# Twelve direct second products of the second layer become block products, with weights and x prepared beside the first layer

## The chip, the cores and the metric

The kernel runs on one core of one Trainium2 chip. A core has a matrix engine (TensorE, PE in the profile, with its weight loads as PEld), three engines for elementwise work (VectorE = DVE, ScalarE = ACT, GpSimd = POOL) and SyncE (SP), which here issues the transfers (DMA). The metric is the time of one execution in device microseconds (us). A time is the median of the runs shown; the profile is of one execution.

## The reference

Causal attention with a decay over 4 x 8 heads of 576 rows and width 64 gives 2304 tokens of width 512. Two layers follow, each 512 to 2048 to 512, with a gate between its two products:

```python
attn_out = _attn_ref(**attn_kwargs)                      # 2304 x 512
h = x @ w_in                                             # first layer
g = s * (r * r) + b                                      # r = max(h, 0)
x = g @ w_out
h = x @ w_in                                             # second layer, other weights
g = np.maximum(h, 0.0) + alpha * np.minimum(h, 0.0)
return g @ w_out
```

The weights arrive as 64-bit floats, handed over as 64-bit integers; everything else is float32.

## The kernel before, in words

**Numbers.** TensorE multiplies operands rounded to a shorter format (fp32r), so each float32 operand is held as a high half (a rounded copy) and a low half (what the copy lost, by a subtraction), and each product is three matmuls: high x high, high x low, low x high. Forming a pair of halves is a copy, mostly by ScalarE, and a subtraction by VectorE or GpSimd.

**Three parts.** Until about 335 us the core computes attention, with the first layer of the first six token blocks (256 tokens each) over the first half of d_ff beside it. From 335 to 601 us it computes the rest of the first layer in "wide" steps (`moe_step` with `big`): one step takes one block of 128 rows of d_ff and 512 tokens (256 for the last block), with 12 matmuls for the first product (L968), then ScalarE's max (L972), VectorE's square and scale (L975), ScalarE's or VectorE's addition of b into the high half of g (L979, L981), VectorE's low half (L985), and 12 matmuls for the second product (L992 for 256 tokens, L995 for 512). There are 56 such steps, 40 of 512 tokens and 16 of 256. From 601 us the second layer runs: three passes over 768 tokens each, and in a pass eight steps p, each a pair of 128-row blocks of d_ff.

**The second layer's first product** (`pair`, L1271) is a 2 x 2 block product done with seven products instead of eight: seven operands of x (sums and differences of quarters), seven of the weights, 7 x 6 matmuls of 384 columns (L1290), and the sums of the seven results by ScalarE's copies and VectorE's additions (L1305, L1311) around the gate (L1314).

**Its second product** has two forms. `flat` (L1366) multiplies directly: 36 matmuls of 512 columns (L1382) a step, with the gate's result split into halves (L1340, L1344). `seconds` (L1153) takes the steps of a chunk (two or four) and makes seven block products of them, 9 matmuls of 256 columns (L1232) for each step and product; it needs combinations of g (L1159), their halves (L1216, L1218), seven weight operands a step, and additions of the results (L1173, L1257). PLAIN = (8, 4, 0) says how many steps of each pass use `flat`: all eight, four, none.

**The second layer's data.** Its weights are unpacked from 64 bits beside the first layer (`keep`, L477: ScalarE L456, VectorE L447, L450, L453) and stored as float32 in DRAM. In the first pass they are fetched again, and `sums_of` (L488) and `outs_of` (L525) form the seven operands of the first product and the halves of the direct one; `mixed_of` (L545), in the second pass, forms the four sums for the block products. Each x leaves `finish_x2` (L1019) as seven operands: split and subtracted in pieces (L1060, L1063, L1070), written to DRAM, and read again.

**The order.** The program is written out by a list scheduler in the kernel (`Scheduler`). Every piece of work is a task with its engine or engines, a modelled cost, the keys it reads and writes, its buffers and a priority (smaller goes first). The scheduler simulates the engines; each engine, when free, takes the ready task of the smallest priority whose buffers are free. Work that may go to VectorE or GpSimd is modelled with a shared port. Buffers come from rings with a fixed number of slots. The elementwise work has the priority EPR = -50, the wide steps 1000 and up, the weights of the second layer 1100 and up. On the chip each engine then runs its list in that order, waiting on semaphores.

## Time and profile before

| | |
|---|---|
| median of 3 runs (981.89 to 985.65) | 985.58 us |
| the profiled execution | 984.31 us |
| its span in the trace | 982.5 us |
| TensorE busy | 965.5 us (98%), 6063 matmuls |
| VectorE, ScalarE, GpSimd busy | 741.0, 529.9, 327.5 us |
| DMA | 219.34 MB, mean 223 GB/s |

The span is from the first to the last instruction that the profile shows; the rest of an execution, 1.8 us here, lies around it. Busy time counts an engine's own instructions only; a busy engine is not by itself the bound. A wait names the instruction that came last before the waiting one could go. A matmul's duration in the timeline is longer than the step from one start to the next, since matmuls overlap; the pace is read from starts.

### The profile page before, as it was taken

To read this page: it belongs to the slowest core of one execution; us is meant where nothing else is said; L and a number is where in the kernel's file an instruction comes from. 1 tells how busy PE (TensorE), PEld (TensorE's weight loads), DVE (VectorE), ACT (ScalarE), POOL (GpSimd) and SP (SyncE) were. 2 spreads that over 40 slices of the span, in tenths; PEclk is the share of its full clock that TensorE was granted. 3 is DMA by queue.
4 is the path that set the end of the run, shared out by engine and by line. 5 is a ranking of instruction groups with operands and counts; after the bars stand their busy time and mean duration, and the time that the engine had idled before them with its cause. 6 is when DMAs were issued, how large, how long until landed. Compare 5 with 4: busy or idle time off the path is not lost. (4 is left out here: it accounts for less than half of the span.)

```text
span 982.5 us, 17732 instructions
## 1 busy us (share of the span) xinstructions
PE 965.5 (98%) x6063; PEld 854.0 (87%) x6063; DVE 741.0 (75%) x1728; ACT 529.9 (54%) x1286; POOL 327.5 (33%) x369
## 2 busy tenths in 40 slices
PE   9999999999999999999999999999999999999997
PEld 6668898997998889988888887888989899999987
DVE  5888876577666488876878688999765779786597
ACT  4777766557566545443534444756535345455441
POOL 3655776375545034222000000454301112333023
PEclk8999999999999999999999999999999999999999
DMA  7764536233522444587798789788688988888645
GB/s 208 227 194 153 180 109 207 83 114 110 186 76 74 151 128 131 160 300 273 267 319 290 264 264 319 270 317 319 244 315 298 307 259 315 316 297 316 225 147 197
DMA packets 96079, 219.34 MB, mean 223 GB/s; under 512 B 8956, under 2 KB 50260, under 8 KB 93012
## 3 DMA queue, kind: packets, MB, share of 16 engines
q1 hardware_dynamic: 95988, 218.20, 65.9%
q8 instruction: 48, 0.79, 0.3%
q14 instruction: 43, 0.35, 0.1%
HBM read 143.45 MB, written 71.18 MB: 218 GB/s over the span
## 5 line engine op out<-in xcount | busy, mean ns | idle before, releaser
L968 PE MATMUL h<-x,i 128*128 128x256 f32 (+1 forms) x864 | 148.3, 320 | 0.3 <-DVE r L975 0.3
L968 PEld LDWEIGHTS h<-x,i 128*128 128x128 f32 x864 | 125.6, 189 | 13.2 <-DVE r L975 0.9
L826 POOL TENSOR_SCALAR e<-e,rec 128x128 f32<-128x128 f32 (+4 forms) x144 | 89.4, 632 | 85.4 <-DVE rec L819 35.5
L1382 PE MATMUL b<-wo,gq 128*128 128x512 f32 x432 | 103.7, 395 | 0.0
L992 PE MATMUL a<-g,o 128*128 128x256 f32 x768 | 103.6, 284 | 0.0
L992 PEld LDWEIGHTS a<-g,o 128*128 128x128 f32 x768 | 95.9, 189 | 1.2 <-issue 0.7
L1382 PEld LDWEIGHTS b<-wo,gq 128*128 128x128 f32 x432 | 80.9, 188 | 18.1
L995 PE MATMUL b<-g,o 128*128 128x512 f32 x384 | 94.4, 391 | 0.6 <-DVE g L985 0.6
L815 ACT ACTIVATE e<-e,ngm 128x128 f32<-128x128 f32 (+4 forms) x144 | 84.3, 587 | 14.8 <-DVE ngm L810 13.1
L1232 PE MATMUL b<-wo,gj 128*128 128x256 f32 x684 | 87.8, 285 | 2.6 <-ACT gj L1216 1.3
L1232 PEld LDWEIGHTS b<-wo,gj 128*128 128x128 f32 x684 | 86.1, 191 | 3.6 <-DVE gj L1218 1.6
L985 DVE SCALAR_TENSOR_TENSOR g<-r,small,g 128x256 fp32r<-128x256 f32 (+1 forms) x104 | 66.6, 640 | 26.8 <-ACT g L979 25.9
L995 PEld LDWEIGHTS b<-g,o 128*128 128x128 f32 x384 | 71.9, 188 | 16.7 <-DVE g L985 1.1
L979 ACT ACTIVATE g<-r,small 128x256 fp32r<-128x256 f32 (+1 forms) x90 | 53.5, 595 | 55.6 <-DVE r L975 22.0
L810 DVE CUSTOM_DVE_ANT_0 e<-s,mask 128x128 f32<-128x128 f32 (+4 forms) x144 | 67.2, 480 | 18.2 <-PE s L792 7.9
L517 POOL TENSOR_TENSOR wi<-sw,wi 128x512 fp32r<-128x512 f32 x12 | 18.3, 1542 | 173.5 <-ACT wi L514 170.1
L866 PE MATMUL t<-ident,e 128*128 128x128 f32 (+1 forms) x400 | 65.5, 277 | 3.5 <-ACT pt L875 2.1
L975 DVE SCALAR_TENSOR_TENSOR r<-h,small,r 128x256 f32<-128x256 f32 (+1 forms) x76 | 42.9, 564 | 34.5 <-ACT r L972 34.0
L877 ACT COPY pt<-t 128x256 f32<-128x256 f32 (+2 forms) x128 | 55.1, 451 | 20.0 <-PE t L866 19.4
L972 ACT ACTIVATE r<-h 128x256 f32<-128x256 f32 (+1 forms) x76 | 34.1, 449 | 53.4 <-PE h L968 53.0
L866 PEld LDWEIGHTS t<-ident,e 128*128 128x128 f32 (+1 forms) x400 | 46.9, 140 | 13.9 <-issue 5.8
L1290 PE MATMUL h<-x,wi 128*128 128x384 f32 x288 | 58.2, 338 | 0.3 <-DVE rt L1340 0.3
...
## 6 DMA issues: line engine op xcount, KB each, us to landing
...
```

The lines of the kernel that those rows point to most:

```text
L810: nc.vector.tensor_tensor_reduce(e.t[0:rows, k0:k1], st_.t[0:rows, 0:w], mask[0:rows, m0:m0 + w], -0.125 if u.f32 else -1.0, init, ALU.add ...
L815: nc.scalar.activation(x, x, AF.Exp, bias=ng[0:rows, col:col + 1], scale=-1.0, accum_out=sm[0:rows, col:col + 1])
L826: eng.tensor_scalar(x, x, rc[0:rows, col:col + 1], 1.0, ALU.mult, ALU.mult)
L866: nc.tensor.transpose(pp.t[0:kw, i * P:i * P + P], e.t[:, P * kb:P * kb + kw], ident)
L877: copy(x.t[0:kw, a:a + PTS * m].rearrange("p (m w) -> p m w", w=PTS)[:, :, 0:w], src)
L968: nc.tensor.matmul(ps.t[:, 0:w], wv[:, wl, kc, :], x.t[:, kc, xl, x0:x0 + w], start=(n == 0), stop=(n == 3 * KC - 1))
L985: nc.vector.scalar_tensor_tensor(g.t[:, 1, 0:w], r.t[:, 0:w], b_t, h, ALU.add, ALU.subtract)
L992: nc.tensor.matmul(acc[u // 2].t[:, T * (u % 2):T * (u % 2) + T], wo.t[:, wl, u * P:u * P + P], g.t[:, gl, 0:w], start=(first and i == 0 a ...
L995: nc.tensor.matmul(acc[u].t[:, 0:w], wo.t[:, wl, u * P:u * P + P], g.t[:, gl, 0:w], start=(first and i == 0), stop=end)
L1232: nc.tensor.matmul(y[t // 2].t[:, T * (t % 2):T * (t % 2) + T], g.t[:, gl, t * P:t * P + P], wop[j // 2].t.rearrange("p a n -> p (a n)").r ...
L1290: nc.tensor.matmul(b.t[:, 0:TH], wi.t[:, wop, wl, k * P:k * P + P], x[:, k, xl, :], start=(start and m == 0), stop=(m == 5), skip_group_ch ...
L1382: nc.tensor.matmul(y.t, G[e, h].t[:, gl, j * P:j * P + P], wo[e].t[:, wl, :], start=(m == 0), stop=(m == 5))
```

## The change

All 24 steps of the second layer take the block form of the second product; `flat`, PLAIN, `outs_of`, `sums_of` and `mixed_of` are gone. The steps are taken in chunks of 2, 2, 4 in the first pass, 4, 4 in the second, 4, 2, 2 in the third.

The seven operands of both weight matrices are formed beside the first layer by `seven_of`, one 256-column operand at a time with a store of its own (256 KB), and read again one by one. Two row pairs of the first matrix stay in SBUF (HELD), two others are formed in the second layer's first pass (LATE); twelve blocks are unpacked at 300 to 360 us already (EARLY).

In the wide steps of the first layer g is formed by ScalarE with four operations (max, square, scale and bias, rounded copy), and the low half is a subtraction on VectorE or GpSimd. The second product of a step is placed MM2 = 3.5 steps behind its first (2.5 before). The cost functions of the scheduler are new (`dv`, `ac`, `pl`).

x stays as float32: in SBUF (`xq`) for the first pass, by way of DRAM for the other two; its seven operands are formed where the pass begins, by operations of two times 384 columns (XOPS).

```diff
@@ -33,10 +33,14 @@
 NXE = 2
 CH = 4
-ZOFF = 0.0
-PLAIN = (8, 4, 0)
-CHUNKS = {1: (4, 6, 8), 2: (0, 4, 6, 8)}
-MIXED = {(1, 0): (3,), (1, 1): (2,), (1, 2): (1,), (1, 3): (0,), (1, 4): (4,), (1, 5): (5,), (1, 6): (6,), (1, 7): (7,)}
+KEEP = 2
+MM2 = 3.5
+LATE = [("wi2", p) for p in (6, 7)]
+EN = (8, 1)
+EA, EB = 300e3, 360e3
...
@@ -345,11 +365,11 @@
+    x2_d = [dram.tile([P, 2, 2, 2, TH], F32, name=f"x2_d{n}") for n in range(3)]
     w2i_d = [dram.tile([P, 7, 2, T], F32R, name=f"w2i_d{n}") for n in range(NP2)]
-    w2b_d = [dram.tile([P, CH, 2, 2, 512], F32R, name=f"w2b_d{n}") for n in range(NP2 // CH)]
-    w2t_d = [[dram.tile([P, CH, 2, T], F32R, name=f"w2t_d{n}_{i}") for i in range(4)] for n in range(NP2 // CH)]
+    w2o_d = [dram.tile([P, 7, CH, 2, T], F32R, name=f"w2o_d{n}") for n in range(NP2 // CH)]
...
@@ -386,16 +406,17 @@
-        "r2": ring("pg2", "r2", 2, [P, T2], F32),
-        "wi2": ring("w2", "wi2", 2, [P, 7, 2, T], F32R),
-        "wo2": ring("w2", "wo2", 4, [P, 2, 512], F32R),
+        "r2": ring("pg2", "r2", 3, [P, T2], F32),
+        "wq": ring("w2", "wq", 14, [P, 2, T], F32R),
+        "wp": ring("wp", "wp", 8, [P, 2, T], F32R),
+                "xq": ring("w2", "xq", 1, [P, 2, 4, TH], F32),
...
@@ -474,102 +501,94 @@
-    def keep(key, fc, prio):
+    SUMS = {"wi2": ((0, (1, 0), (1, 1), ALU.add), (2, (0, 0), (1, 0), ALU.subtract), (1, 0, (0, 0), ALU.subtract), (3, (0, 1), 1, ALU.subtract)),
+    WHOLE = {"wi2": ((0, 0), (0, 1), (1, 1)), "wo2": ((0, 0), (1, 0), (1, 1))}
...
+    def seven_of(key, p, prio, late=False):
...
+            fc, c = 2 * p + e, cb[e % len(cb)]
+            if (key, fc) in EARLY:
+                kc.append((K, "f", e))
+                task(("sp", kb_of(P * 2048), lambda e=e, fc=fc: load(piece(e).bitcast(F32), w2f_d[key, fc])), r=[((key, fc), "f"), "w2"], w=[kc[e]], bufs=[c], prio=prio)
+            else:
+                kc.append((unpack(key, fc, prio, c, after=["w2"], raw=R["raw" if late or e == 0 else "rw"].buf(), view=lambda e=e: piece(e)), "v"))
+
...
+            task([("dvp", dv(n), lambda: f(nc.vector)), ("pool", pl(n), lambda: f(nc.gpsimd))], r=r, w=w, bufs=bufs, prio=prio)
+        for dst, x, y, op in SUMS[key]:
+            both(T, [ka(x), ka(y)], [ka(dst)], cb + [sw], lambda e, dst=dst, x=x, y=y, op=op: e.tensor_tensor(at(dst), at(x), at(y), op))
+        out = {}
+        for o in ([x[0] for x in PRODUCTS] if late else range(7)):
+            x = WHOLE[key][o] if o < 3 else o - 3
+            b = [sw] if o > 2 else [cb[x[0] % len(cb)]]
+            s = R["wq"].buf()
+            hk, lk = (K, "hi", o), (K, "lo", o)
+            task([("act", ac(T, False), lambda s=s, x=x: nc.scalar.copy(s.t[:, 0, :], at(x))),
+                  ("dvp", dv2(T), lambda s=s, x=x: nc.vector.tensor_copy(s.t[:, 0, :], at(x)))], r=[ka(x)], w=[hk], bufs=b + [s], prio=prio)
+            both(T, [ka(x), hk], [lk], b + [s], lambda e, s=s, x=x: e.tensor_tensor(s.t[:, 1, :], at(x), s.t[:, 0, :].bitcast(F32), ALU.subtract))
+            dst = w2i_d[p][:, o] if key == "wi2" else w2o_d[p // CH][:, o, p % CH]
+            task(("sp", kb_of(P * 2048), lambda dst=dst, s=s: rdma(dst, s.t)), r=[hk, lk], w=[(key[:2], "7", p, o)], bufs=[s], prio=prio)
+            out[o] = (s, [hk, lk])
+        return out
...
@@ -997,12 +1016,31 @@
+        def t_g(f, o, key, rr=(), **k):
+            task(("act", ac(w, False, len(k)), lambda: nc.scalar.activation(o(), r_of(), f, **k)), r=[(K, "r")] + list(rr), w=[(K, key)], bufs=[r, g], prio=epr)
+
+        def g_lo(eng):
+            eng.tensor_tensor(g.t[:, 1, 0:w], r_of(), g_hi().bitcast(F32), ALU.subtract)
+        AK = ("acc", name, fc >= HF if not big else 0)
+        if big:
+            task(("act", ac(w), t_a), r=[(K, "h")] + PG, w=[(K, "r")], bufs=[ps, r], prio=epr)
+            t_g(AF.Square, r_of, "r")
+            t_g(AF.Identity, r_of, "r", [("const", 0), ("const", 1)], scale=s_t, bias=b_t)
+            t_g(AF.Copy, g_hi, "hi")
+            task([("dvp", dv(w), lambda: g_lo(nc.vector)), ("pool", pl(w), lambda: g_lo(nc.gpsimd))], r=[(K, "r"), (K, "hi")], w=[(K, "lo")], bufs=[r, g], prio=epr)
+            task(("pe", 12 * mm, t_mm2), r=[(K, "hi"), (K, "lo")] + OK, w=[AK], bufs=[g, wo] + acc, prio=pr2)
+            return AK
...
@@ -1033,53 +1071,28 @@
+                task([("act", ac(n), lambda o=out_, i=in_: nc.scalar.copy(o(), i())), ("dve", dv(n), lambda o=out_, i=in_: nc.vector.tensor_copy(o(), i()))],
+                     r=[AK, "w2"], w=[("xq", 0, dm // 2 * 2 + h) for h in range(2)], bufs=[a, XQ[0]], prio=epr)
...
@@ -1091,6 +1104,8 @@
+    XOPS = ((0, 0), (3, 0, 1, 0), (4, 0, 3, 0), (1, 2), (5, 1, 3, 1), (2, 3), (6, 2, 2, 0))
...
@@ -1101,57 +1116,66 @@
+            xq = R["xq"].buf() if n else XQ[0]
+            pr = epr if n == 0 else base + 16 * n - 8
+            if n:
+                task(("sp", kb_of(P * 12288), lambda xq=xq, blk=blk: load(xq.t, x2_d[blk].rearrange("p k e h t -> p k (e h) t"))), r=x2k[blk] + ["w2"], w=[("xq", n, q) for q in range(4)], bufs=[xq], prio=pr)
+            for i, op in enumerate(XOPS):
...
+                if len(op) > 2:
+                    task([("dvp", dv(2 * TH), lambda xq=xq, op=op: nc.vector.tensor_tensor(xq.t[:, :, op[1], :], xq.t[:, :, op[2], :], xq.t[:, :, op[3], :], ALU.subtract)),
...
+                task(("act", ac(2 * TH, False), lambda hi=hi, q=q, xq=xq: nc.scalar.copy(hi(), xq.t[:, :, q, :])), r=[("xq", n, q)] + (["px"] if i >= 5 else []),
+                     w=[("xslot", i)], bufs=[b, xq], prio=pr)
+                task([("dvp", dv(2 * TH), lambda lo=lo: lo(nc.vector)), ("pool", pl(2 * TH), lambda lo=lo: lo(nc.gpsimd))], r=[("xq", n, q)], w=[("xslot", i)], bufs=[b, xq], prio=pr)
...
-                        task(("sp", kb_of(P * 14336), lambda wi=wi, p=p: rdma(wi.t, w2i_d[p])), r=[("w2i", p)], w=ki, bufs=[wi], prio=z - 6)
+                if p in ready:
+                    wi = ready.pop(p)
+                elif n == 0 and ("wi2", p) in LATE:
+                    wi = seven_of("wi2", p, z - 8, True)
...
-                plain = pi < PLAIN[n]
-                if plain and (n != 1 or pi > 1):
-                    wo, ko = outs_of(p, n, z - 6)
-                G[p] = pair(n, p, z, xop, wi, ki, step_, bank, small_bufs, epr, plain)
-                if plain:
-                    flat(n, p, G[p], wo, ko, z + 2.9, Y, pi == NP2 - 1, rows, epr)
+                    wi = {}
+                    for i, (o, _, _, _) in enumerate(PRODUCTS):
+                        wi[o] = R["wq"].buf(), [("w2il", n, p, o)]
+                        task(("sp", kb_of(P * 2048), lambda b=wi[o][0], p=p, o=o: rdma(b.t, w2i_d[p][:, o])), r=[("wi", "7", p, o)], w=wi[o][1], bufs=[wi[o][0]], prio=z - 6 + 0.1 * i)
+                if pi >= NP2 - KEEP:
+                    ready[p] = wi
+                G[p] = pair(n, p, z, xop, wi, step_, bank, small_bufs, epr)
+                if pi + 1 in CHUNKS[n]:
                     k = CHUNKS[n].index(pi + 1)
+                    seconds(n, ps[CHUNKS[n][k - 1]:pi + 1], z + 2.0, G, Y, u2, pi == NP2 - 1, epr, n == len(order) - 1, rows)
...
@@ -1183,24 +1207,12 @@
+            wop, wk = [], []
+            for p in ps:
+                wb = R["wp"].buf()
+                wop.append(wb)
+                wk.append([(K, "w", i, p)])
+                task(("sp", kb_of(P * 2048), lambda wb=wb, s=OPERAND[bn], p=p: rdma(wb.t, w2o_d[c][:, s, p % CH])), r=[("wo", "7", p, OPERAND[bn]), "px"], w=wk[-1], bufs=[wb], prio=zi - 5)
...
@@ -1455,15 +1421,24 @@
+
+    def keeps(n):
+        for _ in range(min(n, len(early))):
+            i = len(EARLY) - len(early)
+            keep(*early.pop(0), 895.0 + i, EA + (EB - EA) * i / len(EARLY))
+    keeps(EN[0])
     for fc in range(HF, NF):
...
+        AK = moe_step(name, fc, x, 0, w, xk + ["wB"], acc, "hk"[cnt[0] % 2], first, last, p, p + MM2, EPR, True)
...
@@ -1483,14 +1458,16 @@
...
-                keep(key, 2 * p + e, 1100.0 + 8 * p)
-    n0 = len(sc.tasks)
+            if (key, p) not in LATE + HELD:
+                seven_of(key, p, 1100.0 + 8 * p)
+    held = {p: seven_of(key, p, 1190.0) for key, p in HELD}
     for fc in hi_f:
```

The order of ScalarE before, steps 46 to 49 of the wide form (`r` and `g` carry the step's number, `h` and `k` are the banks of the first product, `raw` is an unpacked weight block):

```order
L972 ACTIVATE r_46_6881<-h_6843 128x512
L456 ACTIVATE raw_6839<-raw_6839,sh_t 128x512
L979 ACTIVATE g_46_6904<-r_46_6881,small 128x512
L972 ACTIVATE r_47_6923<-k_6891 128x512
L456 ACTIVATE raw_6888<-raw_6888,sh_t 128x512
L979 ACTIVATE g_47_6945<-r_47_6923,small 128x512
L456 ACTIVATE raw_6907<-raw_6907 128x512
L972 ACTIVATE r_48_6966<-h_6932 128x512
L979 ACTIVATE g_48_6987<-r_48_6966,small 128x512
L972 ACTIVATE r_49_7004<-k_6974 128x512
```

and now, at the same steps (`wq` is an operand of the weights, `rw` and `raw` blocks being unpacked, `xq` the float32 x):

```order
L1026 ACTIVATE g_46_7074<-r_46_7002 128x512
L551 CAST wq_7097<-sw_6981 128x256
L991 ACTIVATE r_48_7100<-h_7061 128x512
L1141 CAST x_7047<-xq_6360 128x2x384
L483 ACTIVATE rw_7024<-rw_7024,sh_t 128x512
L1026 ACTIVATE r_47_7051<-r_47_7051 128x512
L1026 ACTIVATE r_47_7051<-r_47_7051,small 128x512
L1026 ACTIVATE g_47_7120<-r_47_7051 128x512
L991 ACTIVATE r_49_7138<-k_7107 128x512
L1026 ACTIVATE r_48_7100<-r_48_7100 128x512
L1141 CAST xs_7161<-xq_6360 128x2x384
L1026 ACTIVATE r_48_7100<-r_48_7100,small 128x512
```

Between two max operations there stood the sum with b and an unpacking; now three operations of g and two others stand there, and copies of weights (L551) and x (L1141) are mixed in.

TensorE at the turn to the second layer, before (`g_55` is the last wide step, `wi` the weight operands, `h`, `k`, `a` the banks of the seven products):

```order
L995 MATMUL b_7036<-g_55_7387,o_0_5508 128x512 x3
L1290 MATMUL h_7427<-x_6925,wi_0_5634 128x384 x6
L1290 MATMUL k_7440<-x_6925,wi_0_5634 128x384 x6
L1290 MATMUL a_7447<-xs_6622,wi_0_5634 128x384 x6
L1290 MATMUL h_7427<-x_7359,wi_0_5634 128x384 x6
L1290 MATMUL a_7447<-x_7359,wi_0_5634 128x384 x6
```

and now (with `wq` for the weights):

```order
L1301 MATMUL h_7514<-x_7047,wq_7360 128x384 x6
L1301 MATMUL k_7527<-x_7047,wq_7371 128x384 x6
L1301 MATMUL a_7535<-xs_7161,wq_7373 128x384 x6
L1014 MATMUL b_7222<-g_54_7507,o_0_5861 128x512 x3
L1014 MATMUL b_7223<-g_54_7507,o_0_5861 128x512 x3
L1014 MATMUL b_7224<-g_54_7507,o_0_5861 128x512 x3
L1014 MATMUL b_7225<-g_54_7507,o_0_5861 128x512 x3
L1014 MATMUL b_7222<-g_55_7521,o_0_6020 128x512 x3
L1014 MATMUL b_7223<-g_55_7521,o_0_6020 128x512 x3
L1014 MATMUL b_7224<-g_55_7521,o_0_6020 128x512 x3
L1014 MATMUL b_7225<-g_55_7521,o_0_6020 128x512 x3
L1301 MATMUL h_7514<-x_7485,wq_7365 128x384 x6
```

The thirteen products of two steps stood behind the last second product of the first layer; now three of them stand ahead of those of steps 54 and 55, and eleven behind.

TensorE at the first second product of the second layer, before (`gq` is the split gate, `wo` the halves of the weights, `b` the result):

```order
L1290 MATMUL k_7440<-xe_0_7435,wi_1_5880 128x384 x6
L1382 MATMUL b_7598<-wo_0_5687,gq_7554 128x512 x3
L1382 MATMUL b_7598<-wo_1_5726,gq_7535 128x512 x3
L1382 MATMUL b_7614<-wo_0_5687,gq_7554 128x512 x3
L1382 MATMUL b_7614<-wo_1_5726,gq_7535 128x512 x3
L1382 MATMUL b_7632<-wo_0_5687,gq_7554 128x512 x3
L1382 MATMUL b_7632<-wo_1_5726,gq_7535 128x512 x3
L1290 MATMUL a_7510<-xe_0_7460,wi_1_5880 128x384 x6
L1382 MATMUL b_7662<-wo_0_5687,gq_7497 128x512 x3
```

and now (`gj` is a combination of gates, `wp` a weight operand, `x` and `xe` hold operands of x):

```order
L1301 MATMUL k_7527<-xe_0_7587,wq_7674 128x384 x6
L1243 MATMUL b_7734<-wp_7589,gj_7716 128x256 x6
L1243 MATMUL b_7735<-wp_7589,gj_7716 128x256 x3
L1301 MATMUL a_7535<-xe_0_7591,wq_7685 128x384 x6
L1243 MATMUL b_7853<-wp_7594,gj_7720 128x256 x6
L1243 MATMUL b_7854<-wp_7594,gj_7720 128x256 x3
L1243 MATMUL b_7853<-wp_7596,gj_7781 128x256 x6
L1243 MATMUL b_7854<-wp_7596,gj_7781 128x256 x3
L1243 MATMUL b_7734<-wp_7601,gj_7783 128x256 x6
L1243 MATMUL b_7735<-wp_7601,gj_7783 128x256 x3
```

Where groups of three 512-column matmuls stood, each with its own two operands, groups of six and three 256-column matmuls stand, nine for each weight operand.

## Rows read from the trace of the kernel before

**Rows 1.** Stretches: us; PE, PEld, DVE, ACT, POOL busy us (count); clock; DMA; GB/s.
```profile
335.00:601.00 266.00, 265.38 (x1346) 225.77 (x1346) 206.06 (x401) 124.22 (x241) 39.03 (x26) 1.00 0.73 241
601.00:806.00 205.00, 202.89 (x1012) 181.33 (x1011) 160.89 (x293) 106.14 (x216) 52.48 (x51) 1.00 0.84 299
806.00:935.00 129.00, 128.74 (x876) 128.33 (x875) 100.25 (x203) 65.96 (x134) 34.24 (x33) 1.00 0.79 283
935.00:982.50 47.50, 39.73 (x312) 38.91 (x310) 39.84 (x85) 15.45 (x34) 16.02 (x16) 0.96 0.53 178
sum 982.50, PE 965.51 PEld 854.00 DVE 740.96 ACT 529.94 POOL 327.55; mean PE 193.10 PEld 170.80 DVE 148.19 ACT 105.99 POOL 65.51
```

**Rows 2.** TensorE's waits: line waited for; us, times, longest us.
```profile
PE t L866 <- ACT pt L875: 2.1, 3, 1.3
...
PE a L1290 <- DVE c L1311: 1.0, 1, 1.0
...
PE b L995 <- DVE g L985: 0.6, 1, 0.6
```

**Rows 3.** The chain of waits, 700 to 760 us and the whole: start us, us.
```profile
713.36 8.40 PE b L1382 x36
...
920.92 7.56 PE b L1232 x63
```

**Rows 4.** Timeline of TensorE's matmuls, 382 to 589 us: start us, us.
```profile
382.63 1.57 PE L968 MATMUL h<-xs,i 128*128 128x256 f32 x12
384.04 1.57 PE L992 MATMUL a<-g,o 128*128 128x256 f32 x12
...
583.36 2.88 PE L968 MATMUL h<-x,i 128*128 128x512 f32 x12
586.08 2.88 PE L995 MATMUL b<-g,o 128*128 128x512 f32 x12
```

**Rows 5.** Groups of instructions, 335 to 601 us: busy us, mean ns, idle before.
```profile
L473 POOL TENSOR_TENSOR i<-cv,i 128x512 fp32r<-128x512 f32 x8 | 13.4, 1674 | 37.6 <-ACT i L470 37.6
...
L1060 ACT CAST so<-o 128x128 fp32r<-128x128 f32 x34 | 9.6, 296 | 16.3 <-DMA x_d<-so 8.2 <-DVE o L1070 6.9 <-ACT so L1060 0.8
...
L470 ACT CAST i<-cv 128x512 fp32r<-128x512 f32 x8 | 4.9, 613 | 0.8 <-DVE cv L453 0.8
...
L517 POOL TENSOR_TENSOR wi<-cf,wi 128x256 fp32r<-128x256 f32 x2 | 1.8, 920 | 0.0
...
L505 DVE TENSOR_TENSOR sw<-sw,cf 128x256 f32<-128x256 f32 x3 | 1.2, 415 | 0.0
...
L514 ACT CAST wi<-cf 128x256 fp32r<-128x256 f32 x2 | 0.8, 408 | 1.6 <-DMA cf<-wi2f_d 1.6
```

**Rows 6.** Groups of instructions, 806 to 935 us.
```profile
L1173 POOL TENSOR_TENSOR o<-o,sw 128x256 f32<-128x256 f32 x6 | 4.7, 798 | 1.7 <-DVE o L1257 0.8 <-DVE sw L1257 0.8
```

**Rows 7.** Timeline of VectorE, then of GpSimd, 388 to 394 us.
```profile
388.48 0.43 DVE L447 TENSOR_SCALAR cv<-raw 128x512 int32<-128x512 int32 x1
...
389.40 0.68 DVE L450 SCALAR_TENSOR_TENSOR cv<-raw,cv 128x512 int32<-128x512 int32 x1
390.12 1.67 DVE L453 SCALAR_TENSOR_TENSOR cv<-raw,cv 128x512 int32<-128x512 int32 x1
...
389.55 1.68 POOL L473 TENSOR_TENSOR o<-cv,o 128x512 fp32r<-128x512 f32 x1 [2.55 <-DVE g L985]
392.52 1.29 POOL L473 TENSOR_TENSOR i<-cv,i 128x512 fp32r<-128x512 f32 x1 [1.28 <-ACT i L470]
```

**Rows 8.** VectorE's groups by line, 335 to 601 us, the largest of 22.
```profile
L985 DVE SCALAR_TENSOR_TENSOR g<-r,small,g 128x512 fp32r<-128x512 f32 (+1 forms) x56 | 39.0, 697 | 14.8 <-ACT g L979 14.4
```

**Rows 9.** Busy time by stretch, 601 to 700 us, columns as in rows 1.
```profile
601.00:650.00 49.00, 46.89 (x238) 41.99 (x237) 42.96 (x83) 32.93 (x70) 18.30 (x17) 1.00 0.85 303
650.00:700.00 50.00, 50.00 (x249) 44.69 (x248) 46.38 (x75) 28.18 (x55) 20.46 (x19) 1.00 0.78 295
```

**Rows 10.** The tile wo, 800 to 983 us: issue ns min/median/max, first and last start.
```profile
L331 SPq DMA_DIRECT2D wo<-w2b_d x34: 359/462/1794, 799.7 to 968.9; - x34
```

More of the change, by code (lines that the diff above doesn't have):

```diff
@@ L286, in act, with dv, dv2, ac @@
     return (80 if psum else 125) + 0.833 * n + 93 * ptr
+def dv(n):
+    return 100 + 1.05 * n
+def dv2(n):
+    return 110 + 0.53 * n
+def ac(n, psum=True, ptr=0):
+    return (140 if psum else 175) + 0.833 * n + 93 * (ptr > 0)
+def pl(n):
+    return 180 + 2.1 * n
 def pool1(n):
@@ L561, in mixed_of @@
[L561 to L572 removed]
+            return (K, name) if name[0] == "t" else ks[int(name[1]) - 1]
@@ new lines, in both, with split @@
+        def both(n, r, w, bufs, f):
+            task([("dvp", dv(n), lambda: f(nc.vector)), ("pool", pl(n), lambda: f(nc.gpsimd))], r=r, w=w, bufs=bufs, prio=prio)
+        def split(n, r, bufs, k, src, hi, lo):
+            task(("act", ac(n, False), lambda: nc.scalar.copy(hi(), src())), r=r, w=[(K, k, "hi")], bufs=bufs, prio=prio)
+            both(n, r + [(K, k, "hi")], [(K, k, "lo")], bufs, lambda e: e.tensor_tensor(lo(), src(), hi().bitcast(F32), ALU.subtract))
+            return [(K, k, "hi"), (K, k, "lo")]
@@ new lines, in outs_of @@
+        for dst, x, y in (("t1", "b12", "b11"), ("t2", "b22", "t1"), ("t3", "b22", "b12"), ("t4", "b21", "t2")):
+            both(T, [qk(x), qk(y)], [qk(dst)], cs + [sw], lambda e, dst=dst, x=x, y=y: e.tensor_tensor(quad(dst), quad(x), quad(y), ALU.subtract))
+        for e in range(2):
+            w = R["wo2"].buf()
+            done = split(512, [ks[e]], [cs[e], w], ("b", e), lambda c=cs[e]: c.t, lambda w=w: w.t[:, 0, :], lambda w=w: w.t[:, 1, :])
+            task(("sp", kb_of(P * 4096), lambda w=w, e=e: rdma(w2b_d[p // CH][:, p % CH, e], w.t)), r=done, w=[("w2b", p, e)], bufs=[w], prio=prio)
@@ L575, in decay_attention_two_moe @@
+        done = split(4 * T, [(K, f"t{i + 1}") for i in range(4)], [sw, st_], "t", lambda: sw.t, lambda: st_.t[:, 0:4, 0, :], lambda: st_.t[:, 0:4, 1, :])
+        for i in range(4):
+            task(("sp", kb_of(P * 2048), lambda i=i: rdma(w2t_d[p // CH][i][:, p % CH], st_.t[:, i])), r=done, w=[("w2t", p, f"t{i + 1}")], bufs=[st_], prio=prio)
     fpool = pools["fpool"][0]
@@ L1018, in finish_pa @@
                  r=[("pas", blk, i)], w=[("pa", blk, i)], bufs=[o], prio=epr)
-    x2k = {n: [[] for _ in range(7)] for n in range(3)}
+    x2k = {n: [] for n in range(3)}
+    XQ = [R["xq"].buf()]
     def finish_x2(name, w, acc, AK, epr, units, pan=None, pab=()):
@@ L1025, in finish_x2 @@
         for i, dm in enumerate((0, 2, 1, 3) if len(acc) == 4 else (0, 2)):
-            o = R["o"].buf()
-            K = ("x2f", name, dm)
+            o = R["o"].buf() if pan is not None else None
             two = len(acc) == 2
@@ L1041, in finish_x2 @@
                      w=[("pb", name, dm)], bufs=[o], prio=epr)
-                task(("dve", dve(w), lambda o=o, a=a: nc.vector.tensor_tensor(o.t, a.t, o.t, ALU.add)),
+                task(("dve", dv(w), lambda o=o, a=a: nc.vector.tensor_tensor(o.t, a.t, o.t, ALU.add)),
                      r=[AK, ("pb", name, dm)], w=parts, bufs=[a, o], prio=epr)
-        for k in range(2):
-            f = [fs[k][0], fs[k + 2][0]]
-            off = [fs[k][1], fs[k + 2][1]]
-            fk = [fs[k][2], fs[k + 2][2]]
+        for d in range(KC if pan is not None else 0):
+            o, at, key = fs[d]
@@ L1269, in seconds, with pair @@
                 leave(0, [1] if end else [0, 1])
-    def pair(n, p, z, xop, wi, ki, step, bank, tmp, epr, plain):
+    def pair(n, p, z, xop, wi, step, bank, tmp, epr):
         fc = [2 * p, 2 * p + 1]
```

329 lines of the change are left out of this document (102 added, 227 removed).

## The prediction

> **What bounds the kernel now.** I read the busy time by stretch first. TensorE is busy 965.5 of 982.5 us, VectorE, the next, 741.0. The cuts are 335 us (attention's last product), 601 us (first product of the second layer), 806 us (from here on all second products are block products) and 935 us (the last long row of them begins): TensorE has 265.4 of the 266 us of the middle stretch, 202.9 of 205 and 128.7 of 129 in the second layer, and only the end, 39.7 of 47.5, has holes [rows 1]. The table of TensorE's waits then names its stalls: fifteen lines, 11.4 us in all, the largest 2.1 us in three pieces [rows 2]; most of what else is missing lies behind the last matmul. So TensorE's stream of instructions sets the end: a matmul taken out is worth its time, if the operands of those left still arrive.
>
> **The change part by part.**
>
> *Second product.* Twelve of the 24 steps compute it directly: 36 matmuls of 512 columns, 8.40 us in the chain of waits. The other twelve already do it by seven block products, 7 x 9 = 63 matmuls of 256 columns, 7.56 us for 63 in a row [rows 3]. The change makes the first kind into the second: 12 x (8.40 - 7.56) = -10.1 us, all of it on the path. The 256-column matmul costs 7.56 / 63 = 120 ns there and (384.04 - 382.63) / 12 = 117.5 ns in the first layer [rows 4], so the ends are -10.1 and 12 x (8.40 - 63 x 0.1175) = -12.0; I take -10.1, the row of the same code.
>
> *The turn to the second layer.* Before, thirteen products of two steps stand behind the last first-layer matmul, and the turn's waits are 0.6, 1.0 and, on three lines not shown, 0.5, 0.4 and 0.3 us: 2.8 [rows 2]. There x was split, written to DRAM and read again; now three products stand ahead of the last two steps' second products, and the splits read an x that, for this first pass, never left SBUF. Ends 0 and -2.8; since eleven products still follow in a row, each behind copies of its bank, I take -1.7.
>
> *g by ScalarE.* In the 56 wide-form steps of the first layer VectorE loses the square and the scale, and GpSimd gets the low half in 39 of them. ScalarE gains a square and a copy: 2 x 0.61 us in each of 40 steps of 512 columns, 2 x 0.41 in 16 of 256 by the copies of [rows 5]: 49 + 13 = 62 us.
>
> *Weights beside the first layer.* For each of the eight row pairs of both matrices: 4 sums, 7 high halves, 7 low halves and 7 stores of 256 columns. In the middle stretch the order has 89 high halves on ScalarE (x 0.41 = 36 us), 95 sums and low halves on VectorE (x 0.42 = 40) and 63 on GpSimd, besides 9 low halves of g of that width (72 x 0.80 = 58 [rows 6]). Gone from ScalarE are 55 casts of x: 9.6 us and 21 x 0.41 = 9. ScalarE comes to 124 + 62 + 36 - 19 = 203 of 266 us. It can carry that: a step's second product stands three first products behind its own, six rows of (586.08 - 583.36) = 2.7 us [rows 4], 16 us, and 8 us behind the release of its buffer, where four operations and a subtraction need about 4. What queues worse than before: behind a scale that waits for its DMA stand all four operations of the next g.
>
> VectorE and GpSimd are tighter, since they exclude each other: GpSimd's subtraction of 389.55 us waits until VectorE's 0.68 us operation ends at 390.08, runs to 391.23, and VectorE's next takes 1.67 instead of 0.68 us [rows 7]. So what they do in SBUF adds up. VectorE: 45 unpackings x (0.43 + 0.68 + 0.68) = 81, low halves of g 10, the 95 above 40, casts and wide operations on x 7: 138. GpSimd: 46 operations of full width (16 conversions, 30 low halves of g) x 1.29 = 59 [rows 7], the 72 above 58, 6 on x of three times 256 columns 14: 131. Together 269 for 266 us. Successive rows overlap, though: VectorE's 22 groups of this stretch, the largest shown, sum to 228 [rows 8] where its busy time is 206, so 138 counts as 124 and the sum is 255, 96%. The nearest rows of so full a stretch: 2.1 us without a matmul from 601 to 650 us, VectorE being 88% busy, and none from 650 to 700 us at 93% [rows 9]. By these, 266 us cost 0 to 266 / 49 x 2.1 = 11 us; nothing can be gained, since TensorE has 0.6 us of holes there. I take 3, nearer the end without waits, because the weights, most of what is added, may be late without anyone waiting for them before 601 us.
>
> *The second layer.* It loses the conversion of the weights, the flat sums and the plain g's halves; it gains 84 low halves and 36 drains of 256 columns on VectorE, and for two of its passes the split of x: 11 operations of three times 256 columns, 11 x 3 x 0.415 = 14 us a pass, and 7 casts on ScalarE. The stretch from 806 to 935 us consists of such steps; VectorE is 100.3 of 129 us busy in it and TensorE misses 0.3 [rows 1]. The splits stand where a pass ends and four steps' block products, 30 us, are still in TensorE's queue, which now takes the next pass's products one at a time between them. Ends: 0, and 28 with nothing hidden; by the row of 0.3 us I take +1.5. SyncE issues 280 loads of 256 KB for 76 of 256 to 1792 KB; at 0.46 us [rows 10] that is 129 of some 370 us. The bytes fall from 205 x 0.299 + 129 x 0.283 + 47.5 x 0.178 = 106 MB [rows 1] to about 87. The last 306 matmuls stand in one row on both sides, so the end is taken as the same.
>
> Sum: -10.1 - 1.7 + 3 + 1.5 = -7.3 us. From the profiled execution's 984.31 us (span 982.5 and 1.8 around it) that gives 977.0. The median of the runs shown, 985.58, is 1.3 above that execution, within the spread of the three (981.89 to 985.65); I leave 977.0.
>
> **The rivals.**
>
> *A, most of the gain goes back in waits of a microsecond* (no change that can be told): g's low half late behind unpackings in the middle stretch, or both turns of a pass waiting for x. For it: 96% of 266 us and the 2.1 us of [rows 9]; against it: none at 93%. The stretch's 11 us in place of 3 gives 985.0.
>
> *B, VectorE and GpSimd run out in the middle stretch* (slower). By their lone times they need 255 to 269 us; the change is slower from where the sum passes 266 by the 7 us gained and 5 more. If GpSimd's operations cost what they show in company (46 x 1.67, 72 x 0.92 and 6 x 3 x 0.92: 160 us [rows 5]) and VectorE's 138, the sum is 298, 32 us over; g's low halves lie in the same two queues, so TensorE would wait for them: 977 + 32 = 1009. Against it: those times contain the waiting for each other, counted twice then, as the 1.68 us at 389.55, of which 1.15 is its own [rows 7].
> The Trainium skill states this as a rule (SBUF — State Buffer, section "SBUF: two separate sides"): the pair of ports that VectorE and GpSimd share is locked for a whole instruction, and the other one blocks. By that rule, the trace agrees, the work added to GpSimd is no free cover for VectorE, which speaks against this change.
>
> *C, the small loads starve the block products.* A 256 KB block serves nine matmuls, 1.08 us. At 283 GB/s one lands every 0.93 us, at the end's 178 GB/s every 1.47 [rows 1], and the 34 blocks of the last row would cost 34 x 0.39 = 13 us: 990. Against it: that mean holds idle queues too, and no wait of TensorE in the table is put down to a DMA.
> The Trainium skill's rule (DMA: Bandwidth & Descriptors, "Bandwidth") is to batch transfers to 1 MiB or more; here 1792 KB become seven times 256. No run here shows one such transfer alone.
>
> *D, more is gained:* 117.5 ns a matmul, no waits at the turn, none added: 984.3 - 12.0 - 2.8 = 969.5.
>
> **How the numbers follow.** Chances: the forecast, 973 to 980.6, 0.61; D and all below 973, 0.13; A 0.14 and C 0.04, between 980.6 and 990.5; B 0.08, above. What a measurement of this kernel can tell from no change is about 0.5%, 4.9 us. So faster (forecast and D) has 0.74, the same (A and C) 0.18, slower (B) 0.08. The range runs from D, 969, to two past A, 987; B and most of C are left out, and a little below.
>
> **What would show it.** Right: 324 more matmuls in about 955 us of TensorE's busy time; 63 block matmuls in 7.6 us from the first pass on; ScalarE near 200 us in the middle stretch, GpSimd over 110, and TensorE's waits there, for g's low half, under 5 us; the turn near 601 us with less than 2 us of waits. Wrong in the first term: 256-column matmuls slower than 120 ns. Wrong in the third: the first product of the second layer later than 604 us, with waits for g from VectorE or GpSimd ahead of it. Wrong in the fourth: waits for x's operands or g's low halves where the passes turn.

## The result

The changed kernel takes 973.67 us (median of 4 runs, 972.01 to 973.99), the kernel before 984.96: ratio 0.9888, 95% interval 0.9864 to 0.9912. The forecast was 977.0, in a range of 969 to 987. The profiled executions are 984.31 and 973.43 us, with spans of 982.5 and 971.6: 10.9 us less.

Busy time by stretch of the changed kernel, as in [rows 1] (us; PE, PEld, DVE, ACT, POOL busy; clock; DMA share; GB/s):

```profile
335.00:601.00 266.00, 265.18 (x1346) 225.95 (x1347) 183.02 (x263) 192.51 (x386) 143.25 (x124) 1.00 0.73 245
601.00:806.00 205.00, 202.26 (x1371) 200.36 (x1370) 163.35 (x316) 107.14 (x214) 50.93 (x43) 1.00 0.76 247
806.00:935.00 129.00, 128.73 (x917) 128.35 (x917) 98.93 (x176) 67.53 (x135) 38.19 (x34) 1.00 0.72 223
935.00:971.60 36.60, 29.16 (x237) 28.33 (x235) 30.78 (x70) 9.67 (x20) 13.53 (x14) 1.00 0.62 192
sum 971.60, PE 954.75 PEld 862.41 DVE 720.01 ACT 596.79 POOL 431.98; mean PE 190.95 PEld 172.48 DVE 144.00 ACT 119.36 POOL 86.40
```

TensorE is as full as before in the middle stretch (265.2 of 266 us) with 143 us of GpSimd where there were 39, and 193 of ScalarE where there were 124. Its sum fell by 965.51 - 954.75 = 10.8 us with 324 more matmuls. Behind 601 us the transfers run at 247, 223 and 192 GB/s instead of 299, 283 and 178.

TensorE's waits behind attention, as in [rows 2]:

```profile
PE b L1243 <- DVE gj L1230: 1.9, 2, 1.1
PE b L1243 <- ACT gj L1228: 1.3, 1, 1.3
PE a L1301 <- ACT a L1316: 1.1, 1, 1.1
...
PE a L1011 <- DVE g L1029: 0.8, 1, 0.8
...
PE a L1301 <- ACT u L1318: 0.6, 1, 0.6
```

The turn's 2.8 us are down to the 0.6 for u. New are 0.8 in the first layer and 1.1 each at 713 us (in the first row) and 744 us (the third), about where the first pass turns into the second. The last two waits of the end, 1.3 and 0.8 (the 0.8 is the rest of the 1.9 in the first row), are the old ones.

Two rows of block products in the chain of waits, as in [rows 3], now in the first pass and at its end:

```profile
640.59 7.55 PE b L1243 x63
...
733.56 7.56 PE b L1243 x63
```

63 matmuls take 7.55 to 7.56 us here too: 120 ns each.

Now the two ends of the second layer on TensorE's timeline (start us, us), first the kernel before, from its first product to its last matmuls, then the changed one, from the fourth product:

```profile
600.80 1.21 PE L1290 MATMUL h<-x,wi 128*128 128x384 f32 x6
...
974.80 2.32 PE L1232 MATMUL b<-wo,gq 128*128 128x256 f32 x18
```

```profile
604.72 1.21 PE L1301 MATMUL h<-x,wq 128*128 128x384 f32 x6
...
964.04 2.31 PE L1243 MATMUL b<-wp,gq 128*128 128x256 f32 x18
```

Three products of 1.04 us stand ahead of the row at 604.72, so the changed kernel's second layer begins, in the count of the old order, at 604.72 - 3.12 = 601.60. Up to there it lost 0.8 us; from there to the last matmul it takes 364.7 us where the other takes 376.3: 11.6 less. Behind the last matmul stand 5.4 us before and 5.2 now.

### The profile page after: what moved, and what is told of

Same layout as the page of the kernel before. It is cut to its first block, busy times and chain, and to the rows that moved or that the text cites. A ratio compares the mean times of both kernels' runs of the same rounds, so it can differ in the third digit from the quotient of the medians.

```text
span 971.6 us, 18825 instructions
## 1 busy us (share of the span) xinstructions
PE 954.7 (98%) x6387; PEld 862.4 (89%) x6387; DVE 720.0 (74%) x1585; ACT 596.8 (61%) x1418; POOL 432.0 (44%) x458
## 4 chain that ended last, share of the span: by engine, by line
PE 88%; DVE 4%; DMA 4%; ACT 2%; issue 1%; SPq 0%; POOL 0%; DVEq 0%; ACTq 0%; POOLq 0%
PE b L1243 17%; PE h L987 12%; PE a L1011 9%; PE a L1301 8%; PE b L1014 7%; PE k L1301 5%; PE h L1301 5%; PE k L987 5%; PE t L938 5%; PE t L885 4%; PE s L810 2%; PE a L1014 2%; PE s L811 2%; PE s L815 2%; PE h L445 2%; DMA raw<-in_wo_dram 1%
## 5 line engine op out<-in xcount | busy, mean ns | idle before, releaser
L1243 PE MATMUL b<-wp,gj 128*128 128x256 f32 x1440 | 180.8, 282 | 3.3 <-DVE gj L1230 1.9
L1243 PEld LDWEIGHTS b<-wp,gj 128*128 128x128 f32 x1440 | 178.4, 188 | 4.1 <-DVE gj L1230 2.5
L1228 ACT CAST gj<-gq 128x384 fp32r<-128x384 f32 x142 | 72.6, 514 | 79.5 <-PE b L1243 69.0
L1230 DVE TENSOR_TENSOR gj<-gq,gj 128x384 fp32r<-128x384 f32 x160 | 98.9, 637 | 15.5 <-ACT gj L1228 14.1
L1183 POOL TENSOR_TENSOR gq<-gq 128x384 f32<-128x384 f32 x33 | 40.1, 1218 | 156.2 <-DVE gq L1341 115.3
L1029 POOL TENSOR_TENSOR g<-r,g 128x512 fp32r<-128x512 f32 (+1 forms) x39 | 53.2, 1368 | 78.2 <-ACT g L1026 72.9
L1183 POOL TENSOR_TENSOR gq<-gq,gq 128x384 f32<-128x384 f32 x38 | 45.3, 1198 | 74.2 <-DVE gj L1230 43.3
L1301 PE MATMUL h<-x,wq 128*128 128x384 f32 x288 | 58.1, 337 | 0.3 <-DVE gq L1341 0.3
L474 DVE TENSOR_SCALAR cv<-raw 128x512 int32<-128x512 int32 x48 | 27.5, 572 | 33.6 <-ACT raw L483 32.2
```

The source lines that it names most:

```text
L1183: both(TH, lambda e: e.tensor_tensor(v(dst), v(x), v(y), op), [("G", n, p, x), ("G", n, p, y)], [("G", n, p, dst)], list(G[p].values()), low)
L1228: task([("act", ac(TH, False), lambda g=g, qv=qv: nc.scalar.copy(g.t[:, 0, :], qv())), ("dvp", dv2(TH), lambda g=g, qv=qv: nc.vector.tenso ...
L1230: task(("dvp", dv(TH), lambda g=g, qv=qv: nc.vector.tensor_tensor(g.t[:, 1, :], qv(), g.t[:, 0, :].bitcast(F32), ALU.subtract)), r=[("G", ...
L1243: nc.tensor.matmul(y[t // 2].t[:, T * (t % 2):T * (t % 2) + T], g.t[:, gl, t * P:t * P + P], wop[k].t[:, wl, :], start=(fresh and k == 0 a ...
L1301: nc.tensor.matmul(b.t[:, 0:TH], wb.t[:, wl, k * P:k * P + P], x[:, k, xl, :], start=(start and m == 0), stop=(m == 5), skip_group_check=True)
```

## The experiments

All ratios are to the kernel before in the same session, with their 95% interval; 973.7 is the changed kernel. The edits are shown in part, and `...` marks what is left out.

**1. All 24 second products direct**, in the kernel before:

```diff
-PLAIN = (8, 4, 0)
-CHUNKS = {1: (4, 6, 8), 2: (0, 4, 6, 8)}
-MIXED = {(1, 0): (3,), (1, 1): (2,), (1, 2): (1,), (1, 3): (0,), (1, 4): (4,), (1, 5): (5,), (1, 6): (6,), (1, 7): (7,)}
+PLAIN = (8, 8, 8)
+CHUNKS = {}
+MIXED = {}
...
```

> The kernel before with all 24 second products direct (12 block ones turned back). Theory (matmul time sets the end): 12 x (8.40 - 7.56) = +10.1 us on the kernel before's 985 us, so about 995 (991 to 999), with TensorE's busy time up by about 10 us. Rival (the gain of the change came from lighter elementwise work, not from fewer columns): with the combinations of g and their halves gone, VectorE and ScalarE have less to do, and the time stays at 985 or falls.

Measured: 988.23 us, ratio 1.0036 (1.0015 to 1.0056): +3.8 in the profiled execution, not +10.1. The chain of waits has the direct steps at their old price in the last pass too:

```profile
886.79 8.40 PE b L1382 x36
...
902.60 8.40 PE b L1382 x36
```

So the term per step stands. Of the other 6.3 us, some 5 lie at the end of the program, where nothing covers the block form. The last pass no longer ends with combinations of g that TensorE waits for (2.4 us), the half clock behind these waits is not seen (1.3, last section), and what is drained behind the last matmul takes 3.8 us instead of 5.4 (1.6). The rest is not put down to anything. The experiment mixed two things, which number 9 takes apart.

**2. g formed on VectorE as before**, in the changed kernel:

```diff
-            t_g(AF.Square, r_of, "r")
-            t_g(AF.Identity, r_of, "r", [("const", 0), ("const", 1)], scale=s_t, bias=b_t)
-            t_g(AF.Copy, g_hi, "hi")
+            task(("dve", dv(w) + 60, t_b), r=[(K, "h"), ("const", 0)], w=[(K, "r")], bufs=[ps, r], prio=epr)
+            task(("act", ac(w, False, 1), lambda: t_c(nc.scalar)), r=[(K, "r"), ("const", 1)], w=[(K, "hi")], bufs=[r, g], prio=epr)
...
```

(The low half goes back to VectorE as well.)

> The changed kernel with g formed as before (VectorE squares and scales and makes the low half, ScalarE adds b); 107 ScalarE operations less. Theory (VectorE and GpSimd exclude each other, and their lone times already fill some 255 of the middle stretch's 266 us): VectorE gains about 51 us, GpSimd loses about 26, the sum goes to 280, so TensorE waits for g's low half: 8 to 14 us more than the changed kernel's 973.7, about 984. Rival (the two engines do work beside each other, VectorE at about 190 of 266 us has room): 973.7 within 2.

Measured: 973.68 us, the same as the changed kernel. The theory's sum fell here. VectorE's timeline (start us, us), then GpSimd's, at one place of the middle stretch:

```profile
368.32 0.69 DVE L477 SCALAR_TENSOR_TENSOR cv<-raw,cv 128x512 int32<-128x512 int32 x1
368.93 0.74 DVE L994 SCALAR_TENSOR_TENSOR r<-h,small,r 128x512 f32<-128x512 f32 x1
369.59 1.13 DVE L480 SCALAR_TENSOR_TENSOR cv<-raw,cv 128x512 int32<-128x512 int32 x1
```

```profile
368.41 1.76 POOL L500 TENSOR_TENSOR i<-cv,i 128x512 fp32r<-128x512 f32 x1 [43.10 <-ACT i L497]
```

L994, the square and scale, reads the bank of the first product in PSUM; it runs beside GpSimd's operation in 0.74 us. L480 and the others read and write SBUF; L480 starts beside the same operation and takes 1.13 us instead of 0.68, as L453 did in [rows 7]. Over the stretch, L994 of 512 columns takes 0.75 us in its 24 cases alone and 0.75 in its 16 beside GpSimd; the low half L1004, all in SBUF, 0.75 in 19 cases alone and 1.19 in 20 beside it (up to 2.33). So VectorE's operations on PSUM don't belong in the sum: 40 x 0.75 + 16 x 0.48 = 38 us come off the 280, and 242 of 266 us is less than the changed kernel has. The Trainium skill (SBUF — State Buffer, "SBUF: two separate sides") names, of VectorE's operations, those with two SBUF inputs or in a two-port mode; the prediction had left this condition out. With it, rule and rows agree: L994 has one input in SBUF and one in PSUM. The omission touches the 280 expected here, which counts L994, and hardly the prediction's 255: of that sum at most the 7 us of casts and operations on x read PSUM. Forming g on ScalarE gained nothing.

**3. All sums and low halves of the weights, and g's low halves, on GpSimd:** in `both` of `seven_of` and in the low half of g

```diff
-[("dvp", dv(n), lambda: f(nc.vector)), ("pool", pl(n), lambda: f(nc.gpsimd))]
+[("pool", pl(n), lambda: f(nc.gpsimd))]
...
```

> The changed kernel with every sum and low half of the weights, and every low half of g, on GpSimd alone. Lone times in the middle stretch: VectorE about 44 us less, GpSimd about 102 more. Theory (exclusion, the sum counts): 255 + 58 = 313 of 266 us, so some 30 to 47 us later, 1004 to 1020. Rival (each engine has its own time): GpSimd at 233 of 266 us is not full, so 973.7 within 3.

Measured: 1006.75 us, ratio 1.0219 (1.0185 to 1.0254), 33 more than the changed kernel. TensorE's waits, then GpSimd's two largest groups from 335 to 650 us (busy us, mean ns, idle before):

```profile
PE h L1301 <- ACT wq L551: 16.8, 1, 16.8
PE k L1301 <- ACT s L1318: 4.7, 1, 4.7
```

```profile
L1029 POOL TENSOR_TENSOR g<-r,g 128x512 fp32r<-128x512 f32 (+1 forms) x56 | 73.0, 1305 | 67.9 <-ACT g L1026 63.1 <-issue 2.6 <-DMA w2o_d<-wq 1.3
L553 POOL TENSOR_TENSOR wq<-sw,wq 128x256 fp32r<-128x256 f32 x56 | 47.6, 871 | 0.0
```

The size is the theory's, but the rows show a second cause: GpSimd stands idle 63 us in front of g's low halves, waiting for ScalarE, and the weights queue behind them in its one list. One of the first products of the second layer then waits 16.8 us for its weights. Behind that wait the clock is low as well: 0.57 of full speed on average from 616 to 640 us. How much is exclusion, how much the list and how much the clock, this run does not tell.

**4. The same work, and x's split, on VectorE alone** (the GpSimd options taken out instead):

```diff
-[("dvp", dv(n), lambda: f(nc.vector)), ("pool", pl(n), lambda: f(nc.gpsimd))]
+[("dvp", dv(n), lambda: f(nc.vector))]
...
```

> The changed kernel with the same work, and the split of x, on VectorE alone; GpSimd keeps only the conversion of the first layer's weights and the combinations of g. VectorE gains about 56 us of lone time in the middle stretch, GpSimd loses about 106. Theory (exclusion): the sum falls from 255 to about 205 of 266 us, the waits for g go, 0 to 1.3 us less: 972.4 to 973.7. Rival (GpSimd is a second pair of hands): VectorE's queue of some 195 us makes g later: 2 to 6 us more, 976 to 980.

Measured: 974.07 us, the same. The middle stretch (columns as above):

```profile
335.00:601.00 266.00, 265.79 (x1358) 225.92 (x1355) 184.25 (x370) 194.37 (x388) 24.35 (x16) 1.00 0.74 250
```

VectorE does 107 operations more in 184 us, where it had 183 with GpSimd beside it: what GpSimd took off it came back as longer operations. GpSimd's 119 us less are worth nothing and cost nothing. The rival's 2 to 6 us did not come.

**5. Six row pairs of the first matrix formed in the first pass:**

```diff
-LATE = [("wi2", p) for p in (6, 7)]
+LATE = [("wi2", p) for p in (2, 3, 4, 5, 6, 7)]
```

> The changed kernel, but six instead of two row pairs of the first matrix are formed in the first pass of the second layer (LATE = 2 to 7). That moves 4 x 11 sums and low halves of 256 columns (18 us of VectorE alone) and two unpackings a pair that is not unpacked early into a stretch where VectorE is idle some 20% of the time. Theory (the block form in the first pass pays only because its operands are formed beside the first layer): waits for wq's low halves in the first pass, 10 to 25 us more, 984 to 999. Rival (elementwise work is hidden wherever it stands, matmul time alone counts): 973.7 within 2.

Measured: 998.26 us, ratio 1.0125 (1.0103 to 1.0146): 25 us more than the changed kernel. TensorE's largest waits, and the stretch that lost most:

```profile
PE b L1243 <- DVE gj L1230: 5.0, 7, 1.2
PE h L1301 <- DVE wq L553: 4.3, 3, 2.2
PE a L1301 <- DVE c L1322: 3.8, 2, 2.3
PE b L1243 <- DVE gj L1229: 2.5, 1, 2.5
```

```profile
650.00:700.00 50.00, 41.48 (x245) 38.38 (x245) 44.24 (x100) 22.95 (x51) 12.70 (x12) 0.93 0.67 218
```

VectorE is 88% busy, wq comes late, and with it c and gj, which stand in the same list; from 650 to 700 us TensorE loses 8.5 us and a clock of 0.93 on top. The early forming of the weights is what lets the block form have the first pass.

**6. Chunks of four steps everywhere:**

```diff
-CHUNKS = ((0, 2, 4, 8), (0, 4, 8), (0, 4, 6, 8))
+CHUNKS = ((0, 4, 8), (0, 4, 8), (0, 4, 8))
-        low = epr + (1.5 if end else 1)
+        low = epr + 0.5
```

> The changed kernel with chunks of four steps everywhere, CHUNKS = ((0, 4, 8), (0, 4, 8), (0, 4, 8)), and the combinations of g at one priority (low = epr + 0.5). The same matmuls, two chunks fewer, so 2 x 21 drains of 256 columns less for VectorE. Theory (what TensorE still waits for behind 601 us, 1.2 + 1.3 + 0.5 + 2.9 us and a tail of 5, comes of VectorE's and ScalarE's work around small chunks): 2 to 6 us less than the changed kernel, 968 to 972. Rival (a chunk of four at the end shows its combinations and results uncovered): no gain, 973 to 978.

Measured: 966.82 us (median of 6, 965.32 to 974.08), ratio 0.9829 (0.9801 to 0.9857): the fastest kernel here. All of TensorE's waits behind attention, and its last matmuls:

```profile
PE a L1011 <- DVE g L1029: 0.8, 1, 0.8
...
PE a L1301 <- ACT u L1318: 0.6, 1, 0.6
...
PE h L1301 <- DVE gq L1341: 0.5, 2, 0.3
```

```profile
949.77 5.92 PE L1243 MATMUL b<-wp,gj 128*128 128x256 f32 x48
955.53 4.48 PE L1243 MATMUL b<-wp,gq 128*128 128x256 f32 x36
```

No wait of the end is left, and the two of 1.1 us at the end of the first pass are gone too. The last matmul ends at 960.0 and the span at 963.3: 3.3 us of drain where there were 5.2. Not all that separates the two profiled executions comes of the edit. The fourth product of the second layer, which stands at 604.72 in the changed kernel, comes 1.7 us earlier:

```profile
603.06 1.21 PE L1301 MATMUL h<-x,wq 128*128 128x384 f32 x6
```

Up to there both kernels have the same instructions in the same order on every engine. What differs is the clock near the start: from 12 to 30 us it is 0.91 here, 0.72 in the changed kernel and 0.81 in the kernel before.

**7. One load of 1 MB for four blocks of 256 KB**, on top of 6:

```diff
-        "wp": ring("wp", "wp", 8, [P, 2, T], F32R),
+        "wp": ring("wp", "wp", 2, [P, CH, 2, T], F32R),
...
-            for p in ps:
-                wb = R["wp"].buf()
...
+            wb, j0 = R["wp"].buf(), min(ps) % CH
...
+            task(("sp", kb_of(P * 2048 * m), lambda wb=wb, s=OPERAND[bn], j0=j0: rdma(wb.t[:, 0:m], w2o_d[c][:, s, j0:j0 + m])), r=[("wo", "7", p, OPERAND[bn]) for p in ps] + ["px"], w=[(K, "w", i)], bufs=[wb], prio=zi - 5)
...
```

> As the chunks of four, with one load of 1 MB for the weight operand of each block product in place of four of 256 KB. By the Trainium skill (DMA: Bandwidth & Descriptors, section Bandwidth) larger transfers come nearer the full rate. Theory (no wait of TensorE is for a weight load, so their size does not matter): the time of the chunks of four within 1.5 us. Rival (small loads cost rate and issue time that someone waits for): 3 us or more less than the chunks of four.

Measured: 969.28 us, ratio 0.9833 (0.9814 to 0.9853), no gain over 6: 2.5 us more by the medians, outside the theory's 1.5 and away from the rival. TensorE now does wait for a load:

```profile
PE b L1240 <- DMA wp<-w2o_d: 2.8, 3, 1.1
```

A block of four must land whole before the first of its 36 matmuls, and two such buffers fill the room of eight small ones; which of the two makes the waits was not tried apart. The Trainium skill's rule (DMA: Bandwidth & Descriptors, "Bandwidth") on batching transfers speaks of their rate; no gain from it shows here, where the small ones were hidden.

**8. The turn of the kernel before, with its weights' low halves as copies on ScalarE:**

```diff
-            both(n, r + [hk], [lk], bufs + [wi],
-                 lambda e, a=a, z=z, src=src: e.tensor_tensor(wi.t[:, a:z, 1, :], src(), wi.t[:, a:z, 0, :].bitcast(F32), ALU.subtract))
+            task(("act", act(n, False), lambda a=a, z=z, src=src: nc.scalar.copy(wi.t[:, a:z, 1, :], src())), r=r + [hk], w=[lk], bufs=bufs + [wi], prio=prio)
...
```

> The kernel before, with the low halves of the weights that its first pass forms replaced by plain copies on ScalarE (the values are wrong by that; work leaves VectorE and GpSimd). Theory (the 2.8 us of waits at its turn and the 2.1 us without matmul from 601 to 650 us came of VectorE's queue, full of weight work): under 1 us of holes from 601 to 650 us, the waits for c, gq and rt gone. Rival (they came of x, which was written to DRAM and read again): the same waits at the same places.

Measured, one run: 986.63 us, which by itself tells nothing. Three of TensorE's waits near the turn, and the stretch behind it:

```profile
PE b L993 <- ACT g L977: 1.9, 1, 1.9
...
PE k L1288 <- DMA xe<-x_d: 1.2, 1, 1.2
...
PE a L1288 <- ACT a L1303: 0.8, 1, 0.8
```

```profile
601.00:650.00 49.00, 46.96 (x239) 42.43 (x238) 37.19 (x79) 36.68 (x79) 5.84 (x7) 1.00 0.89 313
```

VectorE has 37 us there instead of 43, and TensorE's holes are still 2.0. The waits for c, gq and rt are gone there, others stand in their place: for the xe that is read back from DRAM, and for ScalarE, which got the copies. Neither theory holds alone; the order around thirteen products in a row has several things that are late by a microsecond.

**9. The second pass direct as well, the third as it was**, in the kernel before:

```diff
-PLAIN = (8, 4, 0)
-CHUNKS = {1: (4, 6, 8), 2: (0, 4, 6, 8)}
+PLAIN = (8, 8, 0)
+CHUNKS = {2: (0, 4, 6, 8)}
```

> The kernel before with the second pass direct in all its eight steps, PLAIN = (8, 8, 0): four block steps turned back, the third pass and its end as they were. Theory (a step's second product costs its matmuls, 8.40 against 7.56 us, and the first experiment's missing 6 us lay in the end of the third pass): 4 x 0.84 = +3.4 us, 988 where the kernel before has 985 (987 to 990), with the last matmul 3.4 us later. Rival (a block step costs about as much as a direct one, once its combinations and drains are counted): within 1 us of the kernel before.

Measured: 988.26 us, ratio 1.0035 (1.0017 to 1.0053): +3.6 by the medians, as the theory has it. The second layer's ends, with the start of its last row of block products:

```profile
600.03 1.21 PE L1290 MATMUL h<-x,wi 128*128 128x384 f32 x6
...
939.48 10.12 PE L1232 MATMUL b<-wo,gj 128*128 128x256 f32 x83
...
977.30 2.32 PE L1232 MATMUL b<-wo,gq 128*128 128x256 f32 x18
```

In the kernel before that row starts here:

```profile
935.72 10.12 PE L1232 MATMUL b<-wo,gj 128*128 128x256 f32 x83
```

979.62 - 600.03 = 379.6 us against 376.3: +3.3 for four steps. But this +3.3 holds two more things, which cancel. Up to the last row it is 339.45 against 334.92, 4.5 us more; TensorE's waits in it are 3.4 us against 2.4, so the four steps' matmuls have some 3.5, near the 3.4 of the theory. From the last row on it is 1.3 us less, since the half clock of the last section is not seen here. The price of a step's matmuls is shown; that a step costs nothing else is not, since the waits moved by 1.0 us.

**10. Chunks of four in the last pass alone:**

```diff
-CHUNKS = ((0, 2, 4, 8), (0, 4, 8), (0, 4, 6, 8))
+CHUNKS = ((0, 2, 4, 8), (0, 4, 8), (0, 4, 8))
```

> The changed kernel with chunks of four in the last pass alone, CHUNKS = ((0, 2, 4, 8), (0, 4, 8), (0, 4, 8)). Theory (the end is set by the combinations of the last chunk of two steps, 2.9 us of waits, and by what is drained behind the last matmul, 5.2 us; with four steps the row is twice as long and the drains half as many): the two waits gone and a tail near 3.3 us, so 4 to 5 us less than the changed kernel, about 969. Rival (the gain of the chunks of four came from the first pass): 972 to 974.

Measured: 970.2 us (969.09 to 970.61), ratio 0.9849 (0.9826 to 0.9871): 3.5 less. At the end one wait is left of the two:

```profile
PE b L1243 <- DVE gq L1230: 1.2, 1, 1.2
```

The drain is 968.4 - 964.7 = 3.7 us. That is the theory's direction with a little less than its 4 to 5 us: one wait stayed, and the drain did not get to 3.3. The second layer starts where it does in the changed kernel (fourth product at 604.68), so the clock of number 6 plays no part here. So about half of number 6 is the end. Of the 8.3 us between the profiled executions of the changed kernel and number 6, 1.7 stand ahead of the fourth product, with the clock, 3.2 are the end as here, and 3.4 came with the first pass and the priority, which were not tried apart.

## Why the prediction was right

The forecast, -7.3 us to 977.0, had the sign, the mechanism and two thirds of the size; it was 3.3 us too high. Against the profiled executions:

| step | forecast | measured | from |
|---|---|---|---|
| second product, 12 steps | -10.1 | -10.1 | 7.55 us for 63; number 9: some 3.5 for the matmuls of four steps |
| the turn | -1.7 | -2.2 | waits 2.8 to 0.6 |
| middle stretch | +3 | +1.3 | see below |
| turns of the passes and the rest of the second layer | +1.5 | +1.9 | waits 2.6 to 4.5 |
| clock near the end | not seen | -1.3 | last section |
| sum | -7.3 | -10.4 | spans: -10.9 |

Of the 0.5 us left, 0.2 is the shorter drain. The clock's 1.3 us are luck as far as the runs tell: no step of the prediction speaks of them, and other kernels with the same two waits show both clocks.

*Second product.* Right to the tenth. The lower bound by 117.5 ns was not reached: the block rows are at 120 ns.

*The turn.* Right, a little small. The reason given, that x was written and read again, is only part: number 8 has one wait for it among others. What each part of the change gave at the turn is not shown.

*g by ScalarE.* The cover was there, as argued: ScalarE has 193 us (203 forecast) and TensorE waits for no ScalarE operation of g in the first layer. But what VectorE is relieved of by it is worth nothing here: with g back on VectorE the time is the same (number 2).

*Middle stretch.* This is the term that was too large. TensorE's stream is 0.80 us later at 601.60, of that 0.17 from attention (the first product behind it starts at 334.90 instead of 334.73); and the 0.62 of the old wait for g, already in the turn's term, is gone. So the stretch cost 0.80 - 0.17 + 0.62 = 1.25, in the table 1.3, of it 0.8 a wait for g's low half. The sum of 255 us is not what was off by much: without the at most 7 us of VectorE that read PSUM it is still 248. The step from how full the two engines are to how late g comes is. Number 2 has 242 us with PSUM left out and waits 1.4 us in this stretch, number 4 about 205 and waits 0.2, the changed kernel 255 and waits 0.8, all at the same time. Below the 266 us the wait does not follow the sum; what sets it, the runs don't show. GpSimd's groups have lengths near those that the rival B took (1.67 and 0.92 us), waiting for VectorE included:

```profile
L1029 POOL TENSOR_TENSOR g<-r,g 128x512 fp32r<-128x512 f32 x30 | 44.6, 1486 | 72.5 <-ACT g L1026 68.1 <-DMA w2o_d<-wq 4.3
L553 POOL TENSOR_TENSOR wq<-sw,wq 128x256 fp32r<-128x256 f32 x19 | 17.5, 932 | 4.4 <-ACT wq L551 4.4
```

B's error was the one named against it: 1486 and 932 ns contain the waiting, which then counted twice.

*Second layer.* Right in sum: the new waits fell about where the first pass turns into the second, 1.1 us at a time, not for loads. One of them, the 1.1 us for gj at 713 us, is for a low half of g's combinations, one of the waits that the prediction named as a sign against this term; it is inside the 1.5 us. No wait of TensorE there is for a DMA, so rival C had nothing to act on.
